# A fused gated linear attention and channel mix on one core: logarithm, sigmoid, key copies, stated buffers and a new order of all work

## The chip, the cores and the metric

The kernel runs on one core of one Trainium2 chip. The metric is the device time of one execution in microseconds (us). The engines are TensorE (PE; its weight loads are shown apart as PEld), VectorE (DVE), ScalarE (ACT), GpSimd (POOL) and SyncE (SP), which issues all the transfers. Each engine works through its own list of instructions in order and waits, where it must, for semaphores of the others.

## The reference, cut to what matters

```python
B, H, S, D = 4, 8, 768, 48                    # attention; C = H * D = 384, d_ff = 1024
mag = np.sqrt(a_re * a_re + a_im * a_im)
scale = np.minimum(mag, 0.999) / (mag + 1e-06)
a_re_n, a_im_n = (a_re * scale, a_im * scale)
for t in range(S):                            # complex state S of D x D per head
    new_re = ar * S_re - ai * S_im
    new_im = ar * S_im + ai * S_re
    S_re, S_im = (new_re + outer(k[t], v[t]), new_im)
    y[:, :, t] = einsum('bhd,bhde->bhe', q[:, :, t], S_re)
# x = y as [B, S, C]; the channel mix:
xk = mu_k * x + (1.0 - mu_k) * x_prev         # x_prev: x one token earlier
xr = mu_r * x + (1.0 - mu_r) * x_prev
k = np.maximum(xk @ w_k, 0.0)
v = k * k @ w_v
r = 1.0 / (1.0 + np.exp(-(xr @ w_r)))
return r * v
```

The inputs have `a_re` between 0.85 and 0.95 and `a_im` around 0 with a spread of 0.1.

## The kernel before, in words

The tokens are cut into 8 units u of 384 (a batch and a half of its sequence), each into 3 chunks of 128 and 6 pieces of 64. All tensors lie with channels on the 128 partitions (3 tiles of 128) and tokens along the rows.

**gate(u)** (phase g) turns the raw factors into decays: a0 takes the positive part of the real part (a Relu into m; for two tiles of u = 0 a max on DVE), its Ln with a small bias `tiny`, and Exp(-Ln) for the ratio ph; a1 makes the logarithm of the magnitude and bounds it; a2 scans the logs along time, keeps the last value, bounds the sum from below by `L_MIN`, and multiplies queries and keys by Exp of the sum (L685, before's line); b0 and b1 do Arctan, a scan of the phase, and two Sin, and multiply again (L730). Units above 0 work on all three tiles at once (128x1152), unit 0 tile by tile (128x384).

**attend(u)** (phase a) makes the attention: `tr` turns keys (PE transposes), copies on ACT bring them to SBUF as `kt` (all 384 columns, and once more 96 of them for heads 6 and 7), `up` multiplies keys and values into the state, `sc` the scores, DVE masks them into `pt`, `y` adds scores and state, and ACT moves y into X with the row sums.

**mix(u)** (phase m) is the channel mix: xm, then a high and a low part (xhi, xlo); `f` (tile z, L388) is a product with w_k, then Relu, Square, and again a high and a low part in one of two hx buffers; `o` (L469) adds the product with w_v, 8 blocks j of 9 matmuls each; three `z` blocks are the product with w_r, each copied from its PSUM bank into zr, and one Sigmoid then runs over all of zr (128x1152). `y = o * r` goes out. Unit 0 uses whole fp32 weights (L384, and 48 of the o products); the others use weights split in two parts, which phases f (fetch), w (convert) and s (split) prepare.

I call products on 128 x 128 weights (z, o, tr) **full** and those on smaller weights (sc, up, y) **part** products; both names are mine. A block is 9 full matmuls of 384 columns.

What sets the order is a table written by hand, `ORDER`: each step of each phase has a place in it, and the plan emits all steps by place, so each engine's list follows it. Buffers are taken from pools in turn (5 PSUM banks `ps`, 4 buffers `r`, 2 `hx`, 3 `x`). The activation functions live in three tables: exp (Exp, Ln), trig (Arctan, Sin), sigmoid; `act` loads another table whenever the next function needs one (L248). At the end a check of all kept statistics (ok, good, n, bad) decides whether a slow path runs, which it doesn't for these inputs.

Of the kernel before, what the change touches and what calls it, by code (L numbers as in the profile page):

```python
# [22 lines left out]
C = H * D  # L23
# [12 lines left out]
YS = 1  # L36
# [132 lines left out]
}  # L169
PIECE = 2  # L170
GP = 2
HB = 2
R_XK = 1
RB = 4
# [1059 lines left out]
```

## Time and profile before

| what | value |
|---|---|
| time, median of 3 runs | 421.72 us (421.2 to 422.78) |
| span of the profiled execution | 420.5 us |
| its own time | not listed apart; the lowest run is 421.2 |
| PE busy | 370.6 us (88%) |
| PEld busy | 333.5 us (79%) |
| DVE busy | 328.6 us (78%) |
| ACT busy | 316.6 us (75%) |
| POOL busy | 8.2 us (2%) |
| PE in the chain that ended last | 63%, ACT 19%, DVE 5% |

The span goes from the first to the last instruction; what a run takes beyond it is about 1 us. Busy shares are averages over stages: until about 124 us PE has little to do and waits for the gates, and from there on it works almost without a gap.

### The profile page before, as it was taken

Reading aid. Unit: us, or ns where it says so; the run is one execution under the profiler, and the core shown is the slowest. Engines: PE = TensorE matmul, PEld = TensorE weight load, DVE = VectorE, ACT = ScalarE, POOL = GpSimd, SP = SyncE. Lnnn points to the kernel's source line nnn. Section 1 sums busy time; section 2 is a strip of 40 time slices with the busy share of each in tenths; the row PEclk is TensorE's granted clock in tenths of the full one; section 3 lists DMA queues with packets and bytes.
Section 4 is the critical chain, followed back from the end, with each engine's and each line's share of the span. In section 5 each row is a group of like instructions: output and inputs, shape, how many; then the busy total and the mean of one; then the engine's idle time right before and its main releaser. Section 6 shows DMA issues by size and latency. Waiting matters only on the chain.

```text
span 420.5 us, 13399 instructions
## 1 busy us (share of the span) xinstructions
PE 370.6 (88%) x5705; PEld 333.5 (79%) x5705; DVE 328.6 (78%) x528; ACT 316.6 (75%) x620; POOL 8.2 (2%) x32
## 2 busy tenths in 40 slices
PE   0018849998999999999999999999999999999992
PEld 0017725776689999999999999899999999999991
DVE  3988899698899989888999789889979694564231
ACT  6999998976998899679987996789776833345221
POOL 6000000000000000000000000000000000000000
PEclk9999969998999999999999999999999999999998
DMA  7998462451444082334343353513140440100101
GB/s 257 412 373 209 133 223 77 89 187 45 142 104 148 8 256 57 86 153 143 82 127 139 133 139 105 228 29 89 49 107 4 105 95 19 53 0 2 57 2 65
DMA packets 22996, 49.72 MB, mean 118 GB/s; under 512 B 4848, under 2 KB 16368, under 8 KB 22928
## 3 DMA queue, kind: packets, MB, share of 16 engines
q1 hardware_dynamic: 22928, 48.78, 37.3%
q8 instruction: 47, 0.77, 0.8%
q14 instruction: 21, 0.17, 0.1%
HBM read 31.06 MB, written 4.72 MB: 85 GB/s over the span
## 4 chain that ended last, share of the span: by engine, by line
PE 63%; ACT 19%; DVE 5%; issue 4%; DVEq 0%; ACTq 0%
PE z L388 25%; PE o L469 17%; PE y L1011 8%; PE up L853 4%; PE sc L970 3%; ACT L248 2%; ACT sq L255 2%; PE tr L821 2%; ACT ph L255 1%; ACT r L255 1%; PE sc L965 1%; ACT r L429 1%; ACT h L433 1%; PE z L384 1%; ACT x L361 1%
## 5 line engine op out<-in xcount | busy, mean ns | idle before, releaser
L388 PE MATMUL z<-x,w 128*128 128x384 f32 x693 | 130.6, 340 | 0.5 <-ACT kt L834 0.4
L388 PEld LDWEIGHTS z<-x,w 128*128 128x128 f32 x693 | 119.4, 188 | 2.7 <-ACT kt L834 0.7
L469 PE MATMUL o<-hx,w 128*128 128x384 f32 x504 | 99.4, 342 | 0.0
L469 PEld LDWEIGHTS o<-hx,w 128*128 128x128 f32 x504 | 86.2, 188 | 1.1
L429 ACT ACTIVATE r<-z 128x384 f32<-128x384 f32 x64 | 30.5, 488 | 32.6 <-PE z L388 28.3
L970 PE MATMUL sc<-g 48*64 48x64 f32 x1200 | 26.1, 228 | 30.9 <-DVE g L730 29.8
L970 PEld LDWEIGHTS sc<-g 48*64 48x64 f32 x1200 | 23.3, 137 | 34.6 <-DVE g L730 30.0
L730 DVE TENSOR_TENSOR g<-g,r 128x768 f32<-128x768 f32 (+1 forms) x24 | 41.5, 1755 | 6.7 <-ACT r L255 6.4
L441 DVE CAST hx<-h 128x384 fp32r<-128x384 f32 x44 | 16.1, 366 | 28.9 <-ACT h L433 17.1
L433 ACT ACTIVATE h<-r 128x384 f32<-128x384 f32 x64 | 33.1, 526 | 2.8 <-DMA out_t<-y 1.6
L255 ACT ACTIVATE sq<-m 128x1152 f32<-128x1152 f32 (+1 forms) x30 | 28.3, 970 | 6.7 <-DVE m L651 4.6
L445 DVE TENSOR_TENSOR hx<-h,hx 128x384 fp32r<-128x384 f32 x56 | 30.4, 553 | 2.2 <-PE z L388 1.5
L248 ACT ACT_TABLE_LOAD x24 | 30.8, 1283 | 1.2 <-PEq L1223 0.8
L361 ACT CAST x<-xm 128x384 fp32r<-128x384 f32 x42 | 21.3, 515 | 11.6 <-DVE xm L353 6.3
L384 PE MATMUL z<-x,wx 128*128 128x384 f32 x66 | 24.4, 524 | 5.4 <-DVE x L347 5.4
L364 DVE TENSOR_TENSOR x<-xm,x 128x384 fp32r<-128x384 f32 x42 | 23.0, 553 | 7.8 <-ACT x L361 7.6
L1011 PE MATMUL y<-q,state 112*48 112x64 f32 (+1 forms) x704 | 25.4, 226 | 3.1 <-ACT xt L1046 1.9
L1011 PEld LDWEIGHTS y<-q,state 112*48 112x48 f32 (+1 forms) x704 | 22.8, 133 | 6.4 <-issue 4.0
L353 DVE SCALAR_TENSOR_TENSOR xm<-dx,mu_sb,xt 128x384 f32<-128x384 f32 x42 | 25.4, 614 | 0.6
L853 PEld LDWEIGHTS up<-v,kt 64*48 64x48 f32 (+1 forms) x1216 | 21.5, 127 | 5.1 <-issue 3.0
L384 PEld LDWEIGHTS z<-x,wx 128*128 128x128 f32 x66 | 13.4, 208 | 14.5 <-issue 7.3
L853 PE MATMUL up<-v,kt 64*64 64x48 f32 (+1 forms) x1216 | 24.0, 217 | 0.0
(89 smaller groups left out, 557.6 us busy)
## 6 DMA issues: line engine op xcount, KB each, us to landing
g<-in_gat SPq DMA_DIRECT2D x18, 768.0 KB, 5.7
raw<-in_w_all SPq DMA_DIRECT2D x9, 767.8 KB, 10.1
g<-in_gat SPq DMA_DIRECT2D x12, 384.0 KB, 8.1
v<-in_vt SPq DMA_DIRECT2D x24, 192.0 KB, 3.5
out_t<-y SPq DMA_DIRECT2D x24, 192.0 KB, 2.5
q<-g SPq DMA_DIRECT2D x84, 48.0 KB, 2.2
q<-g SPq DMA_DIRECT2D x28, 144.0 KB, 3.1
q<-g SPq DMA_DIRECT2D x40, 72.0 KB, 2.3
```

The source lines that it names most:

```text
L248: nc.scalar.add_instruction(mybir.InstLoadActFuncSet(name=nc.get_next_instruction_name(), act_func_set_id=n, engine=mybir.EngineType.Activ ...
L255: nc.scalar.activation(out=out, in_=in_, func=func, **kw)
L384: nc.tensor.matmul(z, lhsT=wx[s[0]][:, s[1]], rhs=hi[which][:, ct], start=ct == 0, stop=ct == NT - 1)
L388: nc.tensor.matmul(z, lhsT=wt[s[0]][:, part, s[1]], rhs=r[which][:, ct], start=n == 0, stop=n == 3 * NT - 1)
L429: nc.scalar.activation(out=t["r", j], in_=t["f", j], func=AF.Relu, scale=1.0 / W_SCALE)
L433: nc.scalar.activation(out=t["h", j], in_=t["r", j], func=AF.Square)
L445: nc.vector.tensor_tensor(out=t["lo", j], in0=t["h", j], in1=t["hi", j].bitcast(F32), op=ALU.subtract)
L469: nc.tensor.matmul(tiles["o", mt], lhsT=w, rhs=r, start=j == 0 and n == 0, stop=j == NJ - 1 and n == len(parts) - 1)
L730: nc.vector.tensor_tensor(out=g[:, d, 2 * i:2 * i + 2], in0=g[:, d, 2:4], in1=t["r"][:, 1 - i, d].unsqueeze(2).to_broadcast([P, k, 2, U]), ...
L853: nc.tensor.matmul(t["up", c, s][i * HR:(KR if i else HR), h * D:(h + 1) * D], lhsT=keys, rhs=V[u][c][r, h * D:(h + 1) * D], start=True, s ...
L970: nc.tensor.matmul(y, lhsT=g[:, 2 * i, q], rhs=g[:, 2 * i + 1, q], start=i == 0, stop=i == 1)
L1011: nc.tensor.matmul(t["y", team][s][rows, h // 2 - team[0], c], lhsT=lhsT[:, cols], rhs=rhs, start=(s, h % 2) not in begun, stop=stop)
```

## The change

Five edits. (1) a0 takes Ln straight from the loaded real part; Relu, the DVE max and `tiny` go. (2) Each z block gets its Sigmoid straight out of the PSUM bank, in place of the copy, and the Sigmoid over all of zr goes. (3) The key copy for a chunk takes 288 columns (heads 0 to 5) in place of 384. (4) The bound `L_MIN` on the cumulated logs goes (the check on the kept value stays). (5) Each buffer is stated by a table, `HOMES`, in place of a pool's turn, and `ORDER` is a new table for all phases; the last o block of unit 7 is emitted tile by tile (`APART`), and weight fetches come in another order.

```diff
-    ("g", 0): (0, 1, 2, 35, 3, 6, 10, 56, 5, 7, 9, 14, 18, 11, 12, 17, 20, 15, 19, 24, 26, 22, 25, 29, 32, 42, 34, 23,
+    ("g", 0): (2, 0, 1, 3, 11, 21, 9, 19, 4, 16, 20, 23, 8, 10, 13, 12, 14, 17, 26, 29, 31, 34, 39, 41, 18, 22, 25,
...
+APART = 1
+BANKS = dict(ps=PB, x=XB, r=RB, hx=HB, kt=KB, pt=PTS, v=VB, g=GB)
...
+    def home(self, slot):
+        tag, n = slot
+        return f"{tag}{self.homes[tag][n] if tag in self.homes else n % BANKS[tag]}"
...
-    def sigmoid(u):
-        op_act(NT * U, lambda: act(zr[u], zr[u], AF.Sigmoid, scale=1.0 / W_SCALE), table=(u + SIG, "sigmoid"), reads=[("zr", u, mt) for mt in range(NT)],
-               writes=[("r", u)], uses=[zr_slot[u]])
...
-                nc.scalar.copy(out=zr[u][:, mt], in_=tiles["z", mt])
+                act(zr[u][:, mt], tiles["z", mt], AF.Sigmoid, scale=1.0 / W_SCALE)
...
+            apart = u == NU - 1 and j >= NJ - APART
...
+            for mts in [(mt,) for mt in range(NT)] if apart else [range(NT)]:
...
-                    nc.scalar.activation(out=t["m"][:, c], in_=G[u][:, c, 0], func=AF.Relu)
...
-                op_act(n + 110, lambda: act(t["m"][:, c], t["m"][:, c], AF.Ln, bias=tiny), table=(u, "exp"),
-                       writes=kk("m", c), uses=[s_ph, s_m])
+                    act(t["m"][:, c], G[u][:, c, 0], AF.Ln)
+                op_act(n, f0, table=(u, "exp"), reads=gk(c, 0), writes=kk("m", c), uses=[s_ph, s_m, s_g])
...
-                op_dve(n, lambda: nc.vector.tensor_scalar(
-                    out=t["m"][:, c], in0=t["m"][:, c], scalar1=L_MIN, scalar2=None, op0=ALU.max),
-                    rate=2, reads=kk("L", c), writes=kk("m", c), uses=[s_m])
...
-                        nc.scalar.copy(out=kt()[:rows, part * C:part * C + C], in_=t["tr", c, part])
+                        nc.scalar.copy(out=kt()[:rows, part * C:part * C + NT * 2 * D].rearrange("p (h x) -> p h x", x=D),
+                                       in_=t["tr", c, part].rearrange("p (h x) -> p h x", x=HR)[:, :, :D])
```

What the new table moves is shown at three places. The first is PE in the middle of a unit's attention, where scores (sc) and values (y) of heads 4 to 7 are multiplied. Before:

```order
L1011 MATMUL y<-pt,v 64x64 x2
L1011 MATMUL y<-pt,v 48x64 x2
L970 MATMUL sc<-g 64x64 x24
L965 MATMUL sc<-q_93 64x64 x12
L469 MATMUL o<-hx,w 128x384 x9
L388 MATMUL z<-x,w 128x384 x9
L1011 MATMUL y<-q_93,state_86 64x64
L1011 MATMUL y<-q_93,state_86 48x64
```

The same place now:

```order
L1030 MATMUL y<-pt,v 48x64 x2
L1030 MATMUL y<-pt,v 64x64 x2
L1030 MATMUL y<-pt,v 48x64 x2
L989 MATMUL sc<-g 64x64 x24
L984 MATMUL sc<-q_91 64x64 x12
L1030 MATMUL y<-q_91,state_85 64x64
L1030 MATMUL y<-q_91,state_85 48x64
```

The full blocks o and z no longer stand between the part products. Over the whole list from the first product with split weights on, a run of part products between two full ones came 34 times, and comes 17 times now.

The second place is ACT around the Sigmoid of unit 0 (zr) and the trig functions of gate 2 (r). Before:

```order
L255 ACTIVATE r<-r,half_pi 128x1152
L255 ACTIVATE r<-r 128x1152
L408 COPY zr<-z 128x384
L559 CAST w<-wx 128x768
L248 ACT_TABLE_LOAD
L255 ACTIVATE zr<-zr 128x1152
L361 CAST x<-xm 128x384 x2
```

And now:

```order
L281 ACTIVATE r<-r,half_pi 128x1152
L460 ACTIVATE h<-r 128x384
L281 ACTIVATE r<-r 128x1152
L387 CAST x<-xm 128x384
L274 ACT_TABLE_LOAD
L281 ACTIVATE zr<-z 128x384
L387 CAST x<-xm 128x384 x2
L281 ACTIVATE zr<-z 128x384
```

The Sigmoid reads the bank z, runs twice here on 384 columns (the third one stands earlier, with table loads of its own), and the copy is gone. On the fast path ACT had 24 table loads and has 37.

The third place is the end of DVE's list: the output products y of unit 7 and the check of the statistics. Before:

```order
L441 CAST hx<-h 128x384 x2
L445 TENSOR_TENSOR hx<-h,hx 128x384 x2
L1128 TENSOR_SCALAR bad<-n 1x1
L486 SCALAR_TENSOR_TENSOR y<-o,zr 128x384 x3
L1131 TENSOR_LOAD bad
```

And now:

```order
L472 TENSOR_TENSOR hx<-h,hx 128x384
L516 SCALAR_TENSOR_TENSOR y<-o,zr 128x384 x2
L722 COPY stat<-ph 128x9
L1142 TENSOR_TENSOR ok<-stat,lim 128x208
L1143 TENSOR_TENSOR ok<-stat,lim 128x208
L1145 TENSOR_REDUCE good<-ok 128x1
L516 SCALAR_TENSOR_TENSOR y<-o,zr 128x384
L1148 TENSOR_SCALAR bad<-n 1x1
```

Two of the three y stand ahead of the last one, and the check, which stood about 70 rows higher, now stands between them.

## Rows read from the trace of the kernel before

**Rows 1.** Windows by stage: length, busy us and count per engine, clock, DMA share, GB/s.
```profile
core 0: us, PE busy (x) PEld busy (x) DVE busy (x) ACT busy (x) POOL busy (x), PEclk, DMA share, GB/s
0.00:29.20 29.20, 0.00 (x0) 0.00 (x0) 20.30 (x39) 25.14 (x50) 6.49 (x18) 1.00 0.94 358
29.20:58.60 29.40, 19.88 (x578) 16.86 (x578) 25.70 (x51) 27.71 (x63) 0.38 (x1) 0.95 0.57 166
58.60:124.20 65.60, 63.07 (x849) 43.84 (x849) 56.50 (x75) 57.46 (x102) 0.00 (x0) 0.94 0.42 124
124.20:184.20 60.00, 59.63 (x1057) 55.96 (x1059) 55.54 (x84) 52.40 (x96) 0.21 (x1) 1.00 0.40 124
184.20:304.20 120.00, 119.77 (x1832) 113.61 (x1828) 104.70 (x162) 102.52 (x198) 0.21 (x1) 1.00 0.37 112
355.70:412.40 56.70, 56.70 (x328) 56.10 (x326) 24.19 (x52) 22.44 (x52) 0.00 (x0) 1.00 0.07 22
```
**Rows 2.** Waits of PE: line, waited for, us in total, times, longest.
```profile
PE sc L970 <- DVE g L730: 29.8, 2, 29.2
PE z L384 <- DVE x L347: 5.4, 1, 5.4
PE y L1011 <- ACT xt L1046: 1.9, 1, 1.9
```
**Rows 3.** Chain of work, pieces in order: start us, us, what.
```profile
124.19 3.39 PE z L388 x18
...
225.69 0.96 PE sc L970 x45
...
227.55 1.96 PE y L1011 x83
...
264.55 0.86 PE sc L970 x45
...
306.76 1.07 PE up L853 x58
307.83 1.77 PE z L388 x9
...
312.43 1.56 PE o L469 x9
313.99 2.15 PE y L1011 x82
```
**Rows 4.** Groups by form on ACT: count, busy us, mean ns, idle before.
```profile
L248 ACT ACT_TABLE_LOAD x24 | 30.8, 1283 | 1.2 <-PEq L1223 0.8
...
L830 ACT COPY kt<-tr 128x384 f32<-128x384 f32 x34 | 16.1, 490 | 1.6 <-PE tr L821 1.6
...
L255 ACT ACTIVATE zr<-zr 128x1152 f32<-128x1152 f32 x8 | 9.3, 1168 | 0.1
```
**Rows 5.** Timeline of ACT: start us, us, instruction.
```profile
70.86 1.15 ACT L622 ACTIVATE m<-g 128x1152 f32<-128x1152 f32 x1
71.91 0.47 ACT L429 ACTIVATE r<-z 128x384 f32<-128x384 f32 x1
72.39 1.28 ACT L248 ACT_TABLE_LOAD   x1
73.69 1.26 ACT L255 ACTIVATE m<-m,tiny 128x1152 f32<-128x1152 f32 x1
74.98 1.16 ACT L255 ACTIVATE ph<-m 128x1152 f32<-128x1152 f32 x1
```
**Rows 6.** Groups by form on DVE: count, busy us, mean ns, idle before.
```profile
L730 DVE TENSOR_TENSOR g<-g,r 128x2304 f32<-128x2304 f32 x12 | 30.7, 2555 | 5.7 <-ACT r L255 5.4
...
L677 DVE TENSOR_SCALAR m<-m 128x1152 f32<-128x1152 f32 x7 | 5.3, 758 | 0.2
```
**Rows 7.** Timeline of the last 12 us: start us, us, instruction.
```profile
409.02 3.39 PE L469 MATMUL o<-hx,w 128*128 128x384 f32 x18
...
412.51 1.49 DVE L486 SCALAR_TENSOR_TENSOR y<-o,zr 128x384 f32<-128x384 f32 x3 [3.25 <-PE o L469]
413.10 2.69 SPq L490 DMA_DIRECT2D out_t<-y  x3
```

More of the change, by code (lines that the diff above doesn't have):

```diff
@@ L183 @@
 FIRST_LOAD = 2
+WHOLE = 1
+APART = 1
+BANKS = dict(ps=PB, x=XB, r=RB, hx=HB, kt=KB, pt=PTS, v=VB, g=GB)
+HOMES = {
+    "g": "01010101",
+    "hx": "0100101010101010010010101010101010101010100110101010110101",
+    "kt": "001010010110110101101101",
+    "ps": (
+        "400123304221232310134213130442431042014043142432111030143223031432321401414324123020010342303410"
+        "413042420434311202321402111041013210412314340202323402342303013410141202432124032403200414241032"
+        "02304432042311003142314141234302402123014033413043110433104023"
+    ),
+    "pt": "01000110100101100101100110011010",
+    "r": (
+        "021301201230131210102123032103210310203021131320211320312230302031231023122323010113210120322330"
+        "32012013010213200301121223120231301311032200310210310213"
+    ),
+    "v": "120310023102103021301210",
+    "x": "021011122021200011201012022102102022120102022102120011021021102",
+}
 ST_X = 0
@@ L238, in tile_kernel @@
     keep = ctx.enter_context(pool("keep"))
[L239 removed]
+    ps = ctx.enter_context(pool("ps", 1, space=PSUM))
     pso = ctx.enter_context(pool("pso", 1, space=PSUM))
@@ L260, in op, with home, bank @@
         plan[0].op(f, reads, writes)
+    def home(slot):
+        return plan[0].home(slot)
+    def bank(slot, name):
+        return ps.tile([P, 512], F32, tag=home(slot), name=name)
     def op_act(n, f, psum=False, **kw):
@@ L293, in tile_kernel @@
     nc.gpsimd.memset(stat, 0.0)
-    tiny = keep.tile([P, 1], F32, name="tiny")
-    nc.gpsimd.memset(tiny, 2.0 ** -60)
     state = [keep.tile([KR, C], F32, name=f"state{i}") for i in range(NS)]
@@ L349, in whole_new, with one @@
                         in1=hi[which][:, ct], op0=ALU.mult, op1=ALU.add)
-                def one(which=which):
-                    xm[which, ct] = mp["t"].tile([P, U], F32, tag="x", name="xm", bufs=3)
+                def one(which=which, sx=sx):
+                    xm[which, ct] = mp["t"].tile([P, U], F32, tag=home(sx), name="xm")
                     nc.vector.scalar_tensor_tensor(
@@ L461, in mul @@
                 else:
-                    h, l = tiles.pop(("hi", j)), tiles.pop(("lo", j))
+                    h, l = tiles["hi", j], tiles["lo", j]
                     parts = (0, h), (1, h), (0, l)
-                for mt in range(NT):
+                for mt in mts:
                     if j == 0:
@@ L471, in second @@
             k = [("h", u, j)] if whole else [("hhi", u, j), ("hlo", u, j)]
-            op_pe(cost, mul, reads=k + [(w_key, W_V + 2 * j)] + [("o", u, j - 1)] * (j > 0),
-                  writes=[("o", u, j)], uses=[so, hs[j]])
+            for mts in [(mt,) for mt in range(NT)] if apart else [range(NT)]:
+                op_pe(cost * len(mts) / NT, lambda mts=mts: mul(mts), writes=[("o", u, j, mt) for mt in mts],
+                      reads=k + [(w_key, W_V + 2 * j)] + [("o", u, j - 1, mt) for mt in mts if j], uses=[so, hs[j]])
         for j in range(NJ + 1):
@@ L490, in store @@
                 nc.sync.dma_start(out=out[b, mt * P:(mt + 1) * P, half * U:(half + 1) * U], in_=tiles["y", mt])
-            op_dve(U, mul, reads=[("o", u, NJ - 1), ("r", u)], writes=[("y", u, mt)], uses=[so, sr, zr_slot[u]])
+            op_dve(U, mul, reads=[("o", u, NJ - 1, mt), ("r", u, mt)], writes=[("y", u, mt)], uses=[so, sr, zr_slot[u]])
             op_dma(196, store, reads=[("y", u, mt)], uses=[sr])
-        return steps + gates * whole + [lambda: sigmoid(u)] + [lambda mt=mt: end(mt) for mt in range(NT)]
+        return steps + gates * whole + [lambda mt=mt: end(mt) for mt in range(NT)]
     with ExitStack() as fast:
-        gp = fast.enter_context(pool("gp", GP))
+        gp = fast.enter_context(pool("gp"))
         tp = fast.enter_context(pool("tp", 1))
-        ap = fast.enter_context(pool("ap", 2))
+        ap = fast.enter_context(pool("ap"))
         xtp = fast.enter_context(pool("xt", 1))
@@ L508, in tile_kernel @@
         hx_slot, upper = [], []
-        for _ in range(HB):
-            x = mp["h"].tile([P, 2, U], F32R, tag="hx", name="hx", bufs=HB)
+        for i in range(HB):
+            hx_slot.append(slot("hx"))
+            x = mp["h"].tile([P, 2, U], F32R, tag=f"hx{i}", name="hx")
             nc.gpsimd.memset(x.bitcast(F32), 0.0)
@@ L818, in f0 @@
                     def f0():
-                        t["tr", c, part] = ps.tile([P, 512], F32, tag="ps", name="tr")[:rows, :C]
+                        t["tr", c, part] = bank(sp, "tr")[:rows, :C]
                         for ct in range(NT):
@@ L838, in turn @@
                           writes=[("tr", u, c, part)], uses=[sp, g_slot[u]])
-                    op_act(U, f1, psum=True, reads=[("tr", u, c, part)], writes=[("kt", u, c, part)], uses=[sp, sk])
+                    op_act(NT * 2 * D, f1, psum=True, reads=[("tr", u, c, part)], writes=[("kt", u, c, part)], uses=[sp, sk])
                     op_act(2 * D, f2, psum=True, reads=[("tr", u, c, part)], writes=[("kt", u, c, 2 + part)], uses=[sp, sk])
@@ L880, in f0 @@
                     def f0():
-                        t["tr", p, part] = ps.tile([P, 512], F32, tag="ps", name="tr")[:, :C].rearrange(
+                        t["tr", p, part] = bank(sp, "tr")[:, :C].rearrange(
                             "p (c r) -> p c r", c=NC)
@@ L955, in f0 @@
                 def f0():
-                    t["sc", team] = sc = [ps.tile([P, 512], F32, tag="ps", name="sc")[:, :m * U // 2].rearrange(
-                        "p (a c q) -> p a c q", a=m, c=NC) for _ in range(2)]
+                    t["sc", team] = sc = [bank(s, "sc")[:, :m * U // 2].rearrange(
+                        "p (a c q) -> p a c q", a=m, c=NC) for s in sp]
                     for a, p in enumerate(team):
@@ L1004, in f0 @@
                 def f0():
-                    t["y", team] = [ps.tile([P, 512], F32, tag="ps", name="y")[:, :m * U // 2].rearrange(
-                        "p (a c q) -> p a c q", a=m, c=NC) for _ in range(2)]
+                    t["y", team] = [bank(s, "y")[:, :m * U // 2].rearrange(
+                        "p (a c q) -> p a c q", a=m, c=NC) for s in sp]
                     begun = set()
@@ L1101, in tile_kernel @@
             run(attend(u), ("a", u))
-            run(mix(u, u == 0), ("m", u))
-            if u == 0:
+            run(mix(u, u < WHOLE), ("m", u))
+            if u == WHOLE - 1:
                 for i in n:
```

74 lines of the change are left out of this document (34 added, 40 removed), and 235 rows, old and new, of the table ORDER.

## The prediction

> **What bounds the kernel now.** I read the windows by stage first, since the shares of the page mix stages that have different limits. [rows 1] show two. From 124.2 us on PE is the bound: it is busy 59.6 of 60 us in one window, 119.8 of 120 in the next, 56.7 of 56.7 near the end, at granted clock 1.00, while DVE and ACT have room (55.5 and 52.4 of 60, then less). Before 124.2 PE is not: it does nothing for 29.2 us, its weight loads fill only 16.9 of 29.4 and 43.8 of 65.6 us, and ACT is busy 25.1 of 29.2, 27.7 of 29.4 and 57.5 of 65.6 us, the highest or nearly so of all. The waits of PE say the same from its side [rows 2]: 29.2 us for the first keys from gate 0, 5.4 us for the first operands of unit 0's mix, and in sum hardly 2 us for anything later. So there are three places to look at: the front, up to the first product with split weights at 124.19 [rows 3]; the PE-bound stretch from there to 412.4, 288.2 us long; and the tail of 8.1 us behind it. Only what ends the front earlier, makes PE's own list shorter, or shortens the tail can show in the time.
>
> **ACT and DVE as a whole.** Start to start, a Relu on 1152 columns costs 71.91 - 70.86 = 1.05 us, a table load 73.69 - 72.39 = 1.30 us [rows 5]; the bias `tiny` costs 1.26 - 1.16 = 0.10. Removed: 7 Relus of 1.05 and one of 0.45 (a third of the columns), 7.8 us; 10 biases, 1.0; 8 Sigmoids of about 1.07 (mean 1168 ns less the overlap of 0.1 that back-to-back rows show) [rows 4], 8.6. The Sigmoid that takes the place of the copy works on the same 384 columns out of the same bank, so I put it at the copy's cost. A key copy takes 490 ns for 384 columns [rows 4]; a quarter fewer columns saves between nothing and 0.12 us, I take 0.08, for 42 copies 3.4 us. Together 20.8 us. Added: 13 table loads (24 to 37), since the z blocks of a unit now need the sigmoid table when their banks are full and exp and trig work lies between: 16.9 us. Net, ACT has about 4 us less of some 300. DVE loses the bound `L_MIN`, 7 times 0.68 us start to start (mean 758 ns) [rows 6] and 3 smaller ones, and two max instructions: some 6 us. In the PE-bound stretch neither is worth anything by itself; there PE's list hides it.
>
> **The front, -4.5 us.** What ends it is the high and low part of unit 1's first operand. I summed both engines' lists up to there, each instruction at its start-to-start time. ACT had 101.8 us of work before it and has 98.1: Relus -3.6, biases -0.6, the Sigmoid of unit 0 -1.1, key copies -0.7, three more table loads +3.9, and 1.6 us of key copies and a weight split that now stand behind it. DVE had 96.2 and has 90.7 (bound and max 2.7, moved 2.8). In the trace the place comes at about 122 us, so ACT stood idle some 20 us in all before it, 4.5 of that for the first load, the rest where PE, DVE and transfers had the turn. If that idle time stays as it is, the front ends 3.7 (ACT) to 5.5 us (DVE) earlier. I take 4.5. The bounds are far apart: half of the other 15 us of idle time could go as well, since attention 0 now stands 7 us of ACT work earlier in the list (some weight conversions went behind it), which gives about -10; and it could be +1, since two weight fetches now go out behind X's own transfers and ACT takes the conversions in order, with everything queued behind them.
>
> **PE's list, -4.2 us.** The same matmuls are issued, but changing between full and part products costs time. A full block behind a full one takes 1.56 us, behind a part run 1.77 [rows 3]: 0.21. A part run behind a full one is longer as well: scores 0.96 against 0.86 behind another part run, values 2.15 against 1.96 [rows 3]: 0.10 to 0.19. So a run of part products between full ones costs 0.31 to 0.40 us beyond its own work. From the first split product on there were 34 such runs, now 17: at 0.33 that is 5.6 us less (5.3 to 6.8). Against it, one `up` (1.07) and three transposes (0.35) that stood before 124.19 now stand behind it: +1.4. Does the rest keep up? I laid the sums of ACT's and DVE's lists against PE's at every operand it reads: before, the smallest lead behind the first few blocks was about 3 us, between 30 and 60 us into the stretch, and now it is about 3 us there too; later it grows past 15 us. So I count no new stall in the forecast, and put a few us into the range.
>
> **The tail, -0.9 us.** Before, the last full products end at 412.4, three y follow one another for 1.49 us, and the third store is issued some 1.6 us behind the last matmul [rows 7]. Now two of the y stand under z's last block, and one y of 0.55 us and one store follow the last matmul: about 0.7 us behind it. The check of the statistics moved in between, 1.3 us on DVE, but there are z (1.56) and three o matmuls (0.52) to cover it; without that cover it would cost up to 1.3.
>
> **Sum.** 420.5 - 4.5 - 4.2 - 0.9 = 410.9 us of span. The median of the runs is 421.72, 1.2 us over the profiled span, so the time is 412.1.
>
> [...] The trace's next ACTIVATE starts 1.30 us after a load starts [rows 5], with 0.02 us ahead of it, so a load costs 1.30 here. [...]
>
> **Rivals.**
> *A, the loads reach PE.* ACT empties PSUM banks in order, so a load ahead of a Relu or Sigmoid holds its bank, and PE waits if ACT has no lead there. Price: up to 13 x 1.30 = 16.9 us, time 412.1 + 16.9 = 429.0, slower than before. It decides where ACT's lead at those places is under 1.3 us. Against it: the 24 loads of before leave no wait of PE in the long stretch beyond some tenths [rows 1, 2], and the smallest lead is about 3 us. For it: leads are sums, not times. Chance 0.07. [...]
> *B, pairs of o blocks starve.* The new list puts two or three o blocks in a row 15 times, where it was twice, and there are still two hx buffers. If DVE sits in a product of 2.56 us [rows 6] when a buffer comes free, PE waits up to 2.56 - 1.56 = 1.0 us. At half of the 13 new places 418.6, at all of them 425.1. Against it: late in the kernel DVE is busy only 24 of 57 us [rows 1]. Chance 0.12, most of it near no change.
> *C, the front gives more.* Half of ACT's idle time goes too: -10 in place of -4.5, time 406.6. For it, the earlier attention 0; against it, that PE's first two long waits [rows 2] run through transfers and a chain over four engines. Chance 0.17.
> *D, the front doesn't move*, since that chain sets it, and only PE's list and the tail shrink: 416.6. Chance 0.09.
> That the order isn't what the table says can't be a rival: the engines' lists have the runs and loads counted above.
>
> **How the numbers follow.** The forecast (408 to 416) has 0.55, C 0.17, D 0.09, B 0.12, A 0.07. The predicted time is 412.1. The range takes in C nearly whole and D and B's milder half: 404.5 to 419.5. About 0.5%, 2.1 us, is what can be told from no change: faster than 419.6 are the forecast, C, D and a little of B, 0.82; within 0.5% most of B, 0.09; slower A and the rest of B, 0.09.
>
> **What would show it.** Right: the first product with split weights near 119.7; about 284 us from there to the last o block; no part run between two full blocks other than the 17; 37 loads of 1283 ns, with PE's waits in the long stretch still under 3 us; one y behind the last matmul. Wrong: a wait of PE on ACT behind a table load (A), of o on DVE hx (B), or a first split product at 124 or later (D), or near 114 (C).

## The result, and the profile of the kernel after

The changed kernel takes 411.83 us (median of 4 runs, 410.64 to 412.38) where the kernel before takes 421.46 us in the same comparison: a ratio of 0.9754, 95% interval 0.9724 to 0.9784, so 2.5% faster. The profiled execution has a span of 408.9 us and a time of 410.64. The predicted time was 412.1 us. Two of its three terms, though, were wrong by several us, in opposite directions, and the third has the right size for another reason; that the time came out is luck in good part, and most of what follows is about that. Three of the kernels below had one or two runs over 1.5% above their fastest; without those b_three stands at 417.44 us, a_relu at 421.66 and a_both at 416.36, and the intervals leave them out.

The windows by stage of the changed kernel, cut where its own stages end: PE's first product at 23.17, the first product of unit 0's mix at 51.14, the first product with split weights at 110.88. The columns are those of [rows 1].

```profile
core 0: us, PE busy (x) PEld busy (x) DVE busy (x) ACT busy (x) POOL busy (x), PEclk, DMA share, GB/s
0.00:23.17 23.17, 0.00 (x0) 0.03 (x1) 15.70 (x28) 19.72 (x43) 6.37 (x17) 1.00 0.92 350
23.17:51.14 27.97, 23.69 (x578) 20.40 (x579) 23.62 (x51) 26.06 (x59) 0.00 (x0) 0.96 0.66 189
51.14:110.88 59.74, 58.78 (x763) 38.59 (x764) 53.07 (x70) 56.69 (x98) 0.19 (x1) 0.93 0.44 147
110.88:170.88 60.00, 58.79 (x1131) 55.86 (x1130) 55.95 (x86) 54.06 (x106) 0.61 (x1) 1.00 0.44 124
170.88:290.88 120.00, 118.52 (x1938) 114.03 (x1935) 103.23 (x157) 104.28 (x199) 0.43 (x1) 1.00 0.43 126
```

Against [rows 1] the first two windows are shorter, 29.20 to 23.17 and 29.40 to 27.97; so is the mix of unit 0, which in the kernel before ended at 120.38 and not at 124.20 (see the correction below):

```profile
58.66:120.38 61.72, 59.67 (x830) 40.73 (x831) 52.87 (x70) 53.58 (x94) 0.00 (x0) 0.94 0.42 128
```

That is 61.72 to 59.74. In the long stretch PE is now idle 1.2 of 60 and 1.5 of 120 us, where it was idle 0.4 and 0.2. The waits of PE name it (line, what it waited for: us in total, times, longest):

```profile
PE tr L903 <- DVE g L748: 23.2, 1, 23.2
PE z L410 <- DVE x L373: 2.2, 2, 1.6
PE y L1030 <- issue: 1.4, 3, 0.9
PE sc L989 <- issue: 0.8, 1, 0.8
PE y L1030 <- ACT xt L1065: 0.8, 1, 0.8
...
PE o L498 <- DVE hx L472: 0.6, 2, 0.4
PE sc L984 <- issue: 0.5, 1, 0.5
```

The two long waits of [rows 2], 29.2 and 5.4 us, are 23.2 and 2.2 (in two pieces). "issue" means that PE stands still and no semaphore that the profile shows holds it. The kernel before had it too,

```profile
PE y L1011 <- issue: 1.8, 3, 1.1
```

but 1.4 of these 1.8 us lie ahead of 50 us. New is that it stands in the long stretch: 2.5 us after, 0.4 before.

The groups of ACT that the change touches (count, busy us, mean ns, idle before):

```profile
L274 ACT ACT_TABLE_LOAD x37 | 47.5, 1283 | 1.5 <-PEq L1243 0.8
...
L848 ACT COPY kt<-tr 128x288 f32<-128x288 f32 x34 | 13.6, 420 | 0.1
L281 ACT ACTIVATE zr<-z 128x384 f32<-128x384 f32 x24 | 11.5, 491 | 18.3 <-PE z L414 17.3 <-PE z L410 0.9
```

As against [rows 4]: 37 loads for 24 at the same 1283 ns, a key copy 420 ns for 490, and the Sigmoid out of the bank takes 491 ns, where the copy took 478.

**A correction first.** The prediction put the end of the front of the kernel before at 124.19 us, from [rows 3]. That row is a piece of the chain, and a piece begins where the chain comes over to PE. The timeline of PE of the kernel before shows two z blocks ahead of it and a short wait between:

```profile
120.38 3.38 PE L388 MATMUL z<-x,w 128*128 128x384 f32 x18
124.19 3.39 PE L388 MATMUL z<-x,w 128*128 128x384 f32 x18 [0.43 <-ACT kt L834]
```

The front ended at 120.38, and the long stretch was 292.0 us, not 288.2. After:

```profile
110.89 3.37 PE L414 MATMUL z<-x,w 128*128 128x384 f32 x18
```

So the change, part by part, read from the two traces:

| | before | after | difference | predicted |
|---|---|---|---|---|
| front, to the first product with split weights | 120.4 | 110.9 | -9.5 | -4.5 |
| long stretch, to the end of the last o product | 292.0 | 290.8 | -1.2 | -4.2 |
| tail | 8.1 | 7.2 | -0.9 | -0.9 |
| span | 420.5 | 408.9 | -11.6 | -9.6 |
| time beyond the span | 1.2 (to 421.72, the median that the prediction had) | 2.9 (to the median) | +1.7 | 0 |

The last line says which executions were profiled, and nothing of the change. Every run whose span is listed took 1.6 to 2.2 us beyond it, where the text ahead of the prediction has about 1: so the profiled execution before took about 422.2 us, a little above its median, and the one after, with 410.64, was the fastest of its four. A term read from one execution each is no better than that: three traces with the front of the changed kernel (after, a_same, a_early) end it at 110.9, 110.2 and 112.0.

### The profile page after: what moved, and what is told of

Same layout as the page of the kernel before. It is cut to its first block, busy times and chain, and to the rows that moved or that the text cites. A ratio compares the mean times of both kernels' runs of the same rounds, so it can differ in the third digit from the quotient of the medians.

```text
span 408.9 us, 13365 instructions
## 1 busy us (share of the span) xinstructions
PE 370.2 (91%) x5705; PEld 336.7 (82%) x5705; DVE 320.2 (78%) x516; ACT 313.0 (77%) x617; POOL 8.9 (2%) x31
## 4 chain that ended last, share of the span: by engine, by line
PE 68%; DVE 16%; ACT 6%; issue 4%; DMA 3%; SPq 2%; DVEq 0%; ACTq 0%
PE z L414 25%; PE o L498 22%; PE y L1030 6%; PE up L872 4%; PE z L410 3%; PE sc L989 3%; PE tr L839 3%; DVE g L748 2%; DVE ph L713 2%; DVE g L703 2%; DVE state L882 1%; DVE m L689 1%; ACT sq L281 1%; DVE w L592 1%; SPq L777 1%
## 5 line engine op out<-in xcount | busy, mean ns | idle before, releaser
L414 PE MATMUL z<-x,w 128*128 128x384 f32 x693 | 127.2, 338 | 0.0
L498 PE MATMUL o<-hx,w 128*128 128x384 f32 x504 | 96.0, 340 | 0.6 <-DVE hx L472 0.6
L274 ACT ACT_TABLE_LOAD x37 | 47.5, 1283 | 1.5 <-PEq L1243 0.8
L410 PE MATMUL z<-x,wx 128*128 128x384 f32 x66 | 26.5, 554 | 2.4 <-DVE x L373 2.2
L989 PE MATMUL sc<-g 48*64 48x64 f32 x1200 | 27.3, 234 | 0.9 <-issue 0.8
L1030 PE MATMUL y<-q,state 112*64 112x64 f32 (+1 forms) x704 | 26.0, 228 | 1.7 <-ACT xt L1065 0.8
L989 PEld LDWEIGHTS sc<-g 48*64 48x64 f32 x1200 | 24.9, 143 | 3.2 <-issue 2.7
L882 DVE TENSOR_TENSOR state<-up,state 112x384 f32<-112x384 f32 x35 | 19.4, 553 | 10.0 <-PE up L872 8.8
L1030 PEld LDWEIGHTS y<-q,state 112*64 112x64 f32 (+1 forms) x704 | 23.3, 135 | 4.7 <-issue 1.7
L903 PE MATMUL tr<-ident,g 128*128 128x128 f32 x18 | 4.8, 430 | 23.6 <-DVE g L748 23.2
L1065 ACT ACTIVATE xt<-y 112x192 f32<-112x192 f32 (+2 forms) x36 | 14.3, 396 | 15.5 <-PE y L1030 14.0
```

The lines of the kernel that those rows point to most:

```text
L274: nc.scalar.add_instruction(mybir.InstLoadActFuncSet(name=nc.get_next_instruction_name(), act_func_set_id=n, engine=mybir.EngineType.Activ ...
L410: nc.tensor.matmul(z, lhsT=wx[s[0]][:, s[1]], rhs=hi[which][:, ct], start=ct == 0, stop=ct == NT - 1)
L414: nc.tensor.matmul(z, lhsT=wt[s[0]][:, part, s[1]], rhs=r[which][:, ct], start=n == 0, stop=n == 3 * NT - 1)
L498: nc.tensor.matmul(tiles["o", mt], lhsT=w, rhs=r, start=j == 0 and n == 0, stop=j == NJ - 1 and n == len(parts) - 1)
L989: nc.tensor.matmul(y, lhsT=g[:, 2 * i, q], rhs=g[:, 2 * i + 1, q], start=i == 0, stop=i == 1)
L1030: nc.tensor.matmul(t["y", team][s][rows, h // 2 - team[0], c], lhsT=lhsT[:, cols], rhs=rhs, start=(s, h % 2) not in begun, stop=stop)
```

## The experiments

The moments in this table are read from the traces, in us; the times are medians. The kernel before stood at 421.46, 420.85, 422.25 and 421.10 in the four comparisons, the changed kernel at 411.83 and, once more, at 411.29.

| kernel | time | first product | unit 0's mix | first split product | end of last o | span |
|---|---|---|---|---|---|---|
| before | 421.46 | 29.2 | 58.7 | 120.4 | 412.4 | 420.5 |
| after | 411.83 | 23.2 | 51.1 | 110.9 | 401.7 | 408.9 |
| b_three: old order, three edits | 417.98 | 28.4 | 57.2 | 117.0 | 406.4 | 413.3 |
| b_four: and the Sigmoid out of the bank | 431.57 | 28.9 | 57.6 | 120.6 | 422.1 | 428.9 |
| a_undo3: new order without the three | 427.40 | 26.8 | 57.1 | 118.4 | 418.1 | 425.2 |
| a_sig: new order, old Sigmoid | 423.63 | 23.2 | 51.4 | 111.8 | 413.9 | 421.0 |
| a_relu: new order, Relu and bias back | 421.96 | 25.6 | 55.9 | 115.7 | 411.8 | 418.9 |
| a_lmin: new order, lower bound back | 413.62 | 24.9 | 52.5 | 111.5 | 403.8 | 410.9 |
| a_loads: 37 more table loads | 444.95 | 26.8 | 56.2 | 120.7 | 434.5 | 441.5 |
| a_shift64: tiny products first (not counted as the first) | 410.94 | 24.3 | 50.8 | 109.7 | 399.9 | 407.4 |
| a_early: check earlier | 410.43 | 23.9 | 52.2 | 112.0 | 402.8 | 408.5 |
| a_arctan: nine loads fewer | 417.03 | 23.7 | 52.0 | 110.9 | 406.1 | 413.2 |
| a_same: the changed kernel again | 411.29 | 23.2 | 51.5 | 110.2 | 401.3 | 408.4 |
| a_both: a_arctan and a_early together | 417.05 | 24.2 | 52.7 | 112.9 | 409.9 | 415.8 |

### Is it the work that was taken out, or the order?

Four kernels, two in the old order and two in the new. The first does three edits in the old order (shown: two of them; the third is the key copy of the change's diff):

```diff
-                    nc.scalar.activation(out=t["m"][:, c], in_=G[u][:, c, 0], func=AF.Relu)
...
-                op_act(n + 110, lambda: act(t["m"][:, c], t["m"][:, c], AF.Ln, bias=tiny), table=(u, "exp"),
+                op_act(n + 110, lambda: act(t["m"][:, c], G[u][:, c, 0], AF.Ln), table=(u, "exp"),
...
-                op_dve(n, lambda: nc.vector.tensor_scalar(
-                    out=t["m"][:, c], in0=t["m"][:, c], scalar1=L_MIN, scalar2=None, op0=ALU.max),
-                    rate=2, reads=kk("L", c), writes=kk("m", c), uses=[s_m])
+                op_dve(n, lambda: None, rate=2, reads=kk("L", c), writes=kk("m", c), uses=[s_m])
```

> The kernel before with its own order, and three of the five edits alone: Ln from the raw real part, no lower bound on the cumulated logs, 288 column key copies. Theory W (less work: the front got shorter because ACT and DVE have less to do before the first product with split weights): some 4.9 us less of ACT and 2.7 us less of DVE work up to there, so the front ends 3 to 5 us earlier and the time is 417 to 419. Theory O (the order: the front got shorter because attention 0 and gate 0 are interleaved in another way): 420.5 to 421.5, at most 1 us less.

It took 417.98 us (415.03 to 422.09), a ratio of 0.9939, interval 0.9905 to 0.9974: 2.9 us, what theory W says. In its trace the front is 3.4 us shorter, also within what W says, the long stretch 2.6 and the tail 1.2; that is 7.2 us, since the profiled execution, with 415.03, was the fastest of ten, so these parts are upper ends. The second adds the Sigmoid out of the bank, still in the old order:

```diff
-        op_act(NT * U, lambda: act(zr[u], zr[u], AF.Sigmoid, scale=1.0 / W_SCALE), table=(u + SIG, "sigmoid"), reads=[("zr", u, mt) for mt in range(NT)],
+        op_act(NT * U, lambda: None, table=(u + SIG, "sigmoid"), reads=[("zr", u, mt) for mt in range(NT)],
...
-                nc.scalar.copy(out=zr[u][:, mt], in_=tiles["z", mt])
+                act(zr[u][:, mt], tiles["z", mt], AF.Sigmoid, scale=1.0 / W_SCALE)
```

> As the run with three edits, and the Sigmoid straight out of the PSUM bank, still in the order of before; table loads go from 24 to 42. ACT gains 18 x 1.30 = 23.4 us of loads and loses 8 x 1.07 = 8.6 us of Sigmoids. If ACT's lead covers loads in the PE-bound stretch (as predicted), 0 to 2 us over the run with three edits. Rival A of the prediction (loads reach PE): up to 15 us over it.

431.57 us, 13.6 us over the run with three edits and 2.6% over the kernel before (interval 2.0 to 3.3%). That is rival A, nearly at its full price: the 14.8 us of ACT work net came out almost whole, most of it in the long stretch (301.5 us for 289.4). With three edits PE has no wait over 0.15 us in that stretch; with the Sigmoid it has 9.1 us of them:

```profile
PE tr L815 <- DVE g L724: 2.5, 2, 2.0
PE y L1006 <- issue: 2.1, 2, 1.4
PE z L386 <- ACT xt L1041: 1.5, 1, 1.5
PE z L386 <- ACT zr L255: 1.2, 1, 1.2
```

Of the 9.1 us, ACT ended 2.8, DVE 4.2, and 2.1 are "issue", which is another matter (below). DVE's share has ACT behind it as well, as far as it is g: in this kernel DVE's g waits 13.3 us for ACT's r, with three edits 6.6.

The third takes the three edits back in the new order, so that little but the order, the buffers and the Sigmoid is left of the change:

```diff
-                    act(t["m"][:, c], G[u][:, c, 0], AF.Ln)
+                    if u == 0 and c.start in (1, 2):
+                        nc.vector.tensor_scalar(out=t["m"][:, c], in0=G[u][:, c, 0], scalar1=0.0, scalar2=None, op0=ALU.max)
+                    else:
+                        nc.scalar.activation(out=t["m"][:, c], in_=G[u][:, c, 0], func=AF.Relu)
+                    act(t["m"][:, c], t["m"][:, c], AF.Ln, bias=tiny)
...
+                    if t["scans", c.start] == len(each(c)):
+                        nc.vector.tensor_scalar(out=t["m"][:, c], in0=t["m"][:, c], scalar1=L_MIN, scalar2=None, op0=ALU.max)
...
```

(Not shown: the key copy, as in the change's diff but the other way round.)

> The changed kernel in its new order, with the three edits taken back: Relu (and max) with the bias before Ln, the lower bound on the cumulated logs, 384 column key copies. Theory W: 3 to 5 us slower than the changed kernel, 415 to 417, the first product with split weights 3 to 5 us later than 110.9. Theory O: 411.5 to 413, the first product with split weights within 1 us of 110.9.

427.40 us: 15.6 us slower than the changed kernel and 1.5% slower than the kernel before (interval 1.2 to 1.8%). Neither theory had that. The front loses 7.5 us and the long stretch 8.9. Its longest waits behind the first product, of which the second and the third lie in the front:

```profile
PE up L880 <- ACT kt L857: 3.1, 3, 1.5
PE z L412 <- DVE x L375: 2.3, 2, 1.4
PE tr L911 <- ACT kt L918: 2.3, 1, 2.3
```

The fourth keeps the new order and the three edits, and takes only the Sigmoid back (in unit 7 two of the three output products read zr ahead of that Sigmoid, since their places are ahead of the third copy; so those two are left without it):

```diff
-                act(zr[u][:, mt], tiles["z", mt], AF.Sigmoid, scale=1.0 / W_SCALE)
+                nc.scalar.copy(out=zr[u][:, mt], in_=tiles["z", mt])
+                copied.append(mt)
+                if len(copied) == NT:
+                    act(zr[u], zr[u], AF.Sigmoid, scale=1.0 / W_SCALE)
```

> The changed kernel with the Sigmoid taken back: each z block is copied from its bank, and one Sigmoid over all of zr follows the third copy. Table loads stay at 36 (37 in the changed kernel), so the new order and not the Sigmoid out of the bank would be what asks for them; ACT gets 8 x 1.07 = 8.6 us more, 1.1 of it in the front. If only work in the front counts: 412 to 413. If ACT binds PE anywhere in the long stretch: 414 to 420.

423.63 us, 11.8 us slower for 8.6 us of ACT; both ranges had less. It has 36 table loads, as expected: the many loads come from the new order and not from the Sigmoid out of the bank. That more is lost than was put on ACT says that place counts beside work: here a unit's first two thirds of zr are only ready behind the third copy. No run parts the two. One place of its timeline shows how a Sigmoid on ACT reaches PE:

```profile
333.52 1.17 ACT L281 ACTIVATE zr<-zr 128x1152 f32<-128x1152 f32 x1
333.86 0.32 PE L875 MATMUL up<-v,kt 64*64 64x48 f32 x4
334.59 0.38 ACT L851 COPY kt<-tr 128x288 f32<-128x288 f32 x1
...
335.54 0.42 ACT L851 COPY kt<-tr 128x288 f32<-128x288 f32 x1
...
336.02 1.23 PE L875 MATMUL up<-v,kt 64*48 64x48 f32 x52 [1.84 <-ACT kt L851]
```

The Sigmoid stands on ACT ahead of four copies and a cast that bring keys to `up`; `up` waits 1.84 us for the last of them.

The four together: the three edits alone give -2.9 us, four edits in the old order +10.7, the new order without the three edits +6.5, and all of it -9.6. Work and order can't be priced apart here. What the last three say is that ACT's work counts in the long stretch, by 8.9 to 12.1 us there, where the prediction had put it at nothing.

### How much of ACT's work counts?

> The changed kernel with the Relu (on DVE for two tiles of unit 0: the max) and the bias ahead of Ln taken back: 8.8 us of ACT work, half of it in the front. Taking back all three edits cost about 16 us. Theory T: 8 to 10 us slower, 420 to 422. Theory L: 3 to 4 us slower, 415 to 416, all of it ahead of the first product with split weights.

The Relu edit alone, taken back in the new order (the first part of the diff above): 421.96 us, 10.1 us slower for 8.8 us on ACT. In the trace 4.9 us are lost in the front, all but 0.1 of it ahead of unit 0's mix, and 5.2 in the long stretch. Theory T, where theory L had all of it in the front.

> The changed kernel with the lower bound on the cumulated logs taken back (right behind the scans): some 6 us of DVE work, 2 of it in the front, none on ACT. If DVE is as tight as ACT: 5 to 7 us slower, 417 to 419. If ACT alone binds: 0 to 2 us slower, in the front, 411.5 to 413.5.

The lower bound alone (the second part of that diff): 413.62 us (411.81 to 415.13), 1.8 us slower for some 6 us on DVE, with ranges that overlap; its span is 2.0 us longer, 0.7 of it in the front, where all of it had been expected. ACT is the tight engine, DVE has some room. What is left of the 15.6 us of all three, 15.6 - 10.1 - 1.8 = 3.7, would be the key copies (42 x 0.08 = 3.4 us), if such shares add up; that part was not run by itself.

And table loads alone, in place of other work:

```diff
-        nc.scalar.add_instruction(mybir.InstLoadActFuncSet(
-            name=nc.get_next_instruction_name(), act_func_set_id=n, engine=mybir.EngineType.Activation, ins=[], outs=[]))
+        for k in ({6: 9, 9: 2, 2: 6}[n], n):
+            nc.scalar.add_instruction(mybir.InstLoadActFuncSet(
+                name=nc.get_next_instruction_name(), act_func_set_id=k, engine=mybir.EngineType.Activation, ins=[], outs=[]))
```

> The changed kernel, with one more table load ahead of each of its table loads (of a table that the next load replaces at once): 37 more, nothing else. Theory L (the prediction's: ACT's lead covers a load in the long stretch): 36 x 1.30 us of ACT work, of which only the 11 or so in the front count, in part: 3 to 8 us slower, 415 to 420. Theory T (the new order is tight: what ACT gets more, the end gets, about one to one, as the Sigmoid's 8.6 us gave 12 us): 35 to 48 us slower, 447 to 460. [...]

444.95 us, 33.1 us slower: 9.8 in the front and 22.9 in the long stretch. That is below theory T's 35 and far above theory L's 8. 36 loads that the program pays for in its course come to 0.92 us each, of 1.30: 0.7 of what ACT gets, the end gets. The load itself costs what the row of the prediction said, two of them back to back on ACT:

```profile
74.42 2.57 ACT L275 ACT_TABLE_LOAD   x2
```

2.57 / 2 = 1.285 us, with nothing between; the mean of the changed kernel's 37 loads is 1283 ns.

Then loads taken away. In gates 2, 4, 5, 6 and 7 the new order has the Arctan of the phase between the exps; behind them it needs fewer loads, nine in all (gate 2 is shown; 4 to 7 go the same way):

```diff
-    ("g", 2): (..., 363, 365, 409, 374, 371, 378, 366, 376, 373, 368, 392, ...
+    ("g", 2): (..., 363, 365, 409, 374, 371, 378, 374.5, 378.3, 378.2, 378.1, 392, ...
```

> The changed kernel with nine table loads fewer: in gates 2, 4, 5, 6 and 7 the Arctan stands behind the two Exp of the scanned logs in place of ahead of them (and the scans of the phase behind the product with the two Exp), as it does in gates 1 and 3. 11.7 us less on ACT. Theory T by the letter (one to one): 399 to 402. Theory M (ACT's work counts one to one only above what PE's own list takes; the long stretch has 3.4 us of standing still left, of which ACT causes about one): -1 to -3 us, 408.5 to 411, most of it in the front, where two of the nine loads are. Rival: the Arctan was put there because ACT would wait for the scans otherwise; then 412 to 416.

417.03 us, 5.7 us slower than the changed kernel beside it (411.29), with 11.7 us less on ACT. Its rival has the sign, though 1 us less than what came, and its reason (ACT waiting for the scans) is not shown. Its front ends at 110.9 as in the changed kernel, so the two loads fewer there bring nothing, and in the long stretch PE has new waits:

```profile
PE y L1030 <- DVE pt L1005: 2.3, 1, 2.3
...
PE z L414 <- ACT r L456: 1.4, 1, 1.4
...
PE z L414 <- DVE x L390: 1.1, 1, 1.1
```

It moved two things, ACT's Arctan and DVE's scans of the phase, which then stand behind a product of 2.55 us, and the wait for the mask pt says that DVE's new place has a part in it; the runs don't part the two. What they settle is that a sum of ACT's work does not give the price either: moved in this way, nine loads fewer cost more than they save.

### What took PE's gain away?

PE stands still for 0.91, 0.77, 0.33 and 0.53 us in the long stretch of the changed kernel with no semaphore to wait for, 2.5 us in sum, always inside a run of part products. One of them (the columns: start us, us, what, and in brackets the idle time ahead):

```profile
135.10 1.38 PE L1030 MATMUL y<-q,state 112*64 112x64 f32 x40
136.41 0.80 PE L1030 MATMUL y<-pt,v 64*64 64x64 f32 x37
138.12 0.42 PE L1030 MATMUL y<-pt,v 64*48 64x64 f32 x11 [0.91 <-issue]
```

Counted from the start of PE's list, the gaps stand ahead of products 1863, 3516, 3768 and 5291. In other kernels with the same list they stand ahead of the same products, though up to 33 us later (1863, 3516 and 5291 in a_undo3, a_relu and a_loads), and each ends 1.2 to 1.6 us behind the end of a transfer of 16384 bytes on the queue that brings instructions. So the suspicion was that PE waits for its own instructions.

```diff
+    pad = ps.tile([P, 512], F32, tag="ps0", name="pad")
+    for _ in range(64):
+        nc.tensor.matmul(pad[:1, :1], lhsT=ones1, rhs=ones1, start=True, stop=True)
```

> The changed kernel with 64 products of 1x1 at the start of PE's list, where PE stands idle for 23 us: 128 more instructions, half of a 16 KB fetch of PE's instructions. In the changed kernel PE stands still for 0.3 to 0.9 us with no semaphore to wait for, ahead of its products 1863, 3516, 3768 and 5291. Theory F (it waits for its instructions): these four gaps go, or move by 64 products in the list, and the time changes by what the new gaps sum to, 409 to 412. Theory N (something in the work at these places): the gaps stay ahead of the same products.

410.94 us (409.12 to 412.49), no difference that can be told. As a test this run failed, for a reason that its trace shows: a product of 1x1 is recorded there as two, with two weight loads, so 256 instructions were added and not 128. This trace has 48 transfers of 16384 bytes on that queue, each of the other thirteen 47: the 256 instructions came to one whole fetch, and then both theories expect the gaps ahead of the same products of the program. There they are: 1863, 5165 and 5291, as in other traces, and one at 3895.

What speaks for theory F is a count that the other traces allow. Number PE's instructions in each trace (products, weight loads and waits for semaphores), and take the number of the one at which PE stands still:

| kernel | product | instruction | remainder by 256 |
|---|---|---|---|
| before | 1735 | 3520 | 192 |
| b_four | 1735, 3260 | 3520, 6592 | 192, 192 |
| after | 1863, 3516, 3768, 5291 | 3776, 7104, 7615, 10687 | 192, 192, 191, 191 |
| a_undo3 | 1863, 3516, 5165, 5291 | 3776, 7104, 10432, 10687 | 192, 192, 192, 191 |
| a_shift64 | 1991, 4023, 5293, 5419 | 4032, 8127, 10688, 10943 | 192, 191, 192, 191 |

In the 13 traces that have such gaps (over 0.15 us, behind 60 us, no semaphore) there are 48, and the remainder is 191 or 192 in every one, at nine places, two in the old list and seven in the new. Work that happened to be slow at a place wouldn't keep to that grid. Theory F holds by this count and by the transfers, not by the shift. (Ahead of 60 us one gap falls off the grid: 1.1 us at remainder 14 in the three kernels of the old order, with a cause that is open.) The place alone doesn't do it: b_three has the list of b_four and no such gap.

### The tail

The changed kernel's last 10 us (start us, us, what):

```profile
401.02 0.69 PE L498 MATMUL o<-hx,w 128*128 128x384 f32 x3
401.10 0.59 DVE L1145 TENSOR_REDUCE good<-ok 128x1 f32<-128x416 f32 x1
401.80 0.56 DVE L516 SCALAR_TENSOR_TENSOR y<-o,zr 128x384 f32<-128x384 f32 x1
401.83 0.19 PE L1147 MATMUL n<-ones,good 128*1 128x1 f32 x2
402.27 0.13 DVE L1148 TENSOR_SCALAR bad<-n 1x1 int32<-1x1 f32 x1
```

One y stands behind the last product, as predicted. But `bad` is only there at 402.40, and the trace's record of PE's branch on it runs from 403.04 to 407.34, 4.3 us. In the kernel before, `bad` was there at 409.26, beside the last 18 products of [rows 7], and the branch ran beside them too.

```diff
-    ("g", 7): (..., 1269, 1279, 1302, 1598, 1308, ...
+    ("g", 7): (..., 1269, 1279, 1302, 1311.5, 1308, ...
...
-        n = ps.tile([P, 512], F32, tag="ps0", name="n")[:1, :1]
+        n = ps.tile([P, 512], F32, tag="ps3", name="n")[:1, :1]
```

> The changed kernel with the check of the statistics earlier: the copy of gate 7's phases into stat stands behind its scans (it stood between the last y), and the check's product takes another PSUM bank, so that good, n and bad stand some 25 us ahead of the end, as in the kernel before. Theory C (the check took back what the split last block gave: in the changed kernel PE's branch on it begins 1.3 us behind the last product and takes 4.3 us): the tail behind the last product goes from 7.2 to some 6.0 us, the time by 1.0 to 1.3 us. Rival: the landing of the last store sets the end all the same, tail 6.9 to 7.2, no change.

The tail behind the last product is 5.7 us where the changed kernel's is 7.2 and, once more, 7.1: theory C. PE's branch begins at 400.17 now, ahead of the last product, and ends at 403.75:

```profile
402.16 0.69 PE L498 MATMUL o<-hx,w 128*128 128x384 f32 x3
402.94 0.56 DVE L516 SCALAR_TENSOR_TENSOR y<-o,zr 128x384 f32<-128x384 f32 x1 [1.57 <-ACT zr L281]
```

The time, 410.43 against 411.29 beside it, is 0.9 us less, which six runs each that spread over 4 us can't tell from none; the spans are alike, since this execution's front was 1.8 us longer. The tail itself is what the trace shows.

> The changed kernel once more, word for word, beside the next three on the same chip: 410.5 to 412.5. If PE waits for its instructions at places that its list sets, the trace has gaps with no semaphore ahead of products 1863, 5165 or 5291 again.

The kernel for comparison: 411.29 us (410.11 to 414.89), in the long stretch with gaps ahead of products 1863, 3768, 5165 and 5291, 1.46, 0.39, 0.34 and 0.53 us.

> The last two edits together: if both do what they are meant to, the sum of their gains, 407 to 410; if one loses, the other's gain less that.

417.05 us: the moved Arctan's loss, and no gain to be seen beside it, though the tail is 5.9 us here as well. No run beats the changed kernel by more than its noise; a_early and a_shift64 lie below it by less than that.

## Why the prediction was right, and where it was wrong

**The time** was right, 412.1 against 411.83, because the front gave 5.0 us more than its term, PE's list 3.0 less, and the median lies 1.7 us further above the profiled span than it did before: -5.0 + 3.0 + 1.7 = -0.3. The first two are errors of the forecast that happen to go against each other, and the third is the choice of the executions that were profiled; so the number was luck, and the mechanism was right in part.

**What the change does to ACT and DVE** held. ACT's busy time fell from 316.6 to 313.0 us (predicted: about 4), DVE's from 328.6 to 320.2 (some 6). The Sigmoid costs about what the copy cost (491 ns for 478), and a load 1.283 us.

**The front, -4.5.** The work was sized well; what was wrong is that the front as a whole goes by a sum of ACT's work with its idle time left as it is. The window up to the first split product, before and then after:

```profile
0.00:120.38 120.38, 79.56 (x1408) 57.63 (x1409) 98.93 (x159) 106.49 (x204) 6.87 (x19) 0.96 0.58 193
```

```profile
0.00:110.89 110.89, 82.48 (x1342) 59.03 (x1342) 92.39 (x147) 102.47 (x197) 6.55 (x18) 0.95 0.60 200
```

ACT's busy time went from 106.5 to 102.5 us (predicted: 3.7 less), DVE's from 98.9 to 92.4 (5.5 less), and ACT's idle time from 13.9 us, which the prediction had at some 20, to 8.4. The step "if that idle time stays as it is" is the one that failed; rival C, a good part of the idle time gone as well, is what happened, with -9.5 for its -10. Where it went shows in the windows: of the 9.5 us, 6.1 are gone ahead of PE's first product, 1.4 between it and unit 0's mix, and 2.0 in that mix. Ahead of the first product ACT now does 19.7 us of work for 25.1 and DVE 15.7 for 20.3; in the mix, where PE is busy 59.7 of 61.7 us and so hardly goes by ACT, ACT does 3.1 us more, 56.7 for 53.6, and its idle time there falls from 8.1 to 3.1. So the change took ACT's work out of the part of the front that waits for it, and put some of it where PE covers it; a sum over the whole front can't see that, and the prediction had PE as no bound anywhere ahead of 124.2. That the moved work alone is the cause was not run by itself: the first product comes at 28.4 with the edits in the old order, at 26.8 with the new order alone, and at 23.2 with both. What the edits are worth there depends on the order: 3.4 us in the old one (b_three), 7.5 in the new one (a_undo3 against after). Rival C's reason, the earlier attention 0, is not shown; with the three edits taken back the new order ends the front only 2.0 us earlier than the old.

**PE's list, -4.2.** Half of the term held. The full blocks got shorter: the time from the start of each run to the start of the next falls for z from 125.3 to 122.0 us and for o from 92.7 to 91.4, together 4.6, for 17 places fewer; 0.21 each had been 3.6. (Not all of it is the places: b_three, with the old list, has these blocks 1.8 us shorter than the kernel before, which leaves 2.8 us, 0.16 each.) The other half, part runs that are 0.10 to 0.19 us cheaper behind another part run, failed: sc went from 19.2 to 20.7 us and y from 27.6 to 29.4; only `up`, with 64 products more, went from 18.1 to 17.7. The price itself was a misreading. The 0.96 and 0.86 of [rows 3] are pieces of the chain of 45 products each, which are cut at other points than the runs are. In the timeline of the kernel before the same 48 scores, first behind a full block,

```profile
225.62 1.03 PE L970 MATMUL sc<-g 48*64 48x64 f32 x48
226.59 0.97 PE L965 MATMUL sc<-q 112*64 112x64 f32 x24
```

and then behind `up`,

```profile
264.38 1.02 PE L970 MATMUL sc<-g 48*64 48x64 f32 x48
265.34 0.97 PE L965 MATMUL sc<-q 112*64 112x64 f32 x24
```

take 0.97 and 0.96 us from start to start, and the values 2.15 (from 313.92 to 316.07) and 2.11 (from 227.33 to 229.44): 0.01 and 0.04 us, not 0.10 and 0.19.

What sc and y gained instead is, by theory F, the wait for instructions. Runs of part products use up instructions at some 22 ns a product (67.9 us for 3072 of them), and at the four gaps of the changed kernel PE went on 1.2 to 1.6 us behind the end of a fetch. Product by product, the changed kernel has seven steps over 0.15 us at instructions of remainder 191 or 192 inside such runs of its long stretch, 4.0 us in all, and the kernel before one, of 0.59; the 3.4 us between them are about what sc and y got longer, 3.3. (The profile's waits show 2.5 of the 4.0 us, since they leave out gaps under 0.15 us and count from the modelled end of the last product.) A rival would be that values which now follow their own scores at once wait for the mask. Behind the scores at 168.17 the mask is ready at 171.36, 0.06 us ahead of the values that read it:

```profile
171.42 1.12 PE L1030 MATMUL y<-pt,v 64*64 64x64 f32 x48
```

In a_same, the same kernel with the mask as close, the same run takes

```profile
171.36 0.92 PE L1030 MATMUL y<-pt,v 64*64 64x64 f32 x48
```

and most of the 0.2 us more in the first stand at its instruction of remainder 192. So the mask is not what made that run longer.

**"In the PE-bound stretch neither is worth anything by itself"** is the sentence that was most wrong, though the time doesn't show it. PE is busy 99% there and yet ACT's work counts: in the long stretch alone the Sigmoid taken back costs 11.3 us, the Relu and bias 5.2, and 25 loads, 32 us of ACT, 22.9. The smallest lead of about 3 us that was worked out from sums of the lists did not protect it. With these edits in the new order PE waits for ACT and DVE by some tenths only, and that made PE's list look like the bound and ACT like an engine with room; what was put back on ACT shows that both are near the bound.

**The tail, -0.9.** The profiles say -0.9, but not for the reason given; that is luck. The three stores of [rows 7] took 2.69 us to issue in that one execution of the kernel before; in b_three, with the same tail:

```profile
406.52 1.49 DVE L484 SCALAR_TENSOR_TENSOR y<-o,zr 128x384 f32<-128x384 f32 x3 [3.24 <-PE o L467]
407.10 1.64 SPq L488 DMA_DIRECT2D out_t<-y  x3
```

That tail is 6.9 us long, and 6.8 in b_four. Against those the new tail, 7.1 to 7.2, gains nothing: what the split last block gave, PE's late branch took back. The prediction asked whether the check's 1.3 us on DVE were covered, and left out the branch behind it.

**Rivals.** A's price was real (b_four: 13.6 us for 18 loads more and 8 Sigmoids over all of zr fewer), and the changed kernel, with its new order, its stated buffers and 37 loads for those 42, does not pay it; which of these does it was not run apart. B did not come: PE waits for hx 0.6 us in all. D did not come.

## What to carry to other kernels

A hand-made order fits the durations that it was made for: in the old order three of the edits gave -2.9 us and a fourth turned that into +10.7, and the new order cost +6.5 without the three, so price an edit and its order together and expect neither part alone to show its share. A busy share of 87 to 90% beside an engine at 99% was not room here; put one known microsecond on the engine and see how much of it reaches the end. And of an engine's waits in the chain, look up in its timeline whether the row is where a stage or a run starts, before a term is measured from it: pieces of the chain gave a front end 3.8 us late and a price that isn't there.

## What the runs showed of the hardware

In runs of products of some 22 ns each TensorE stood still for 0.2 to 1.5 us with no semaphore to wait for, at remainder 191 or 192 by 256 of its own instruction count in all 48 cases behind 60 us, and went on 1.2 to 1.6 us behind the end of a 16 KB transfer of instructions; the author reads it as a wait for these instructions. From start to start a block of nine products on split weights mostly took 1.56 us behind a like block, and mostly 1.64 to 1.77 us behind smaller weights; putting the small products together gained 2.8 to 4.6 us on these blocks and lost 3.3 in sc and y. A copy of 288 columns out of PSUM took 420 ns and one of 384 took 490; a Sigmoid out of PSUM took 491 ns and the copy of as many columns 478. PE's branch over the slow path took 3.3 to 4.6 us in all fourteen traces, and the branches of the other engines 0.04 to 0.07.
